# Where the weight preparation stands between two experts: second weight behind all row transposes, last row's split behind the next comparison, sums of squares later

## The chip, the core and the metric

The kernel runs on one core of one Trainium2 chip. Five engines of the core work side by side, each through its own list of instructions in a fixed order: TensorE (PE, matrix products; the load of its stationary operand is listed as PEld), VectorE (DVE), ScalarE (ACT), GpSimd (POOL) and SyncE (SP). DMA queues move data; here SP issues the weight loads and the transposes, POOL the gathers and scatters by row. The metric is the device time of one execution in microseconds (us). An instruction that must wait holds up everything behind it in its engine's list.

## What is computed

Attention of 8 batches with 8 heads over 576 positions comes first; its result, 4608 tokens of 512 values, then goes through a layer of 8 experts. Each expert takes the 576 tokens that a greedy choice over all logits gives to it, and computes two matrix products:

```python
def _moe_ref(x, w_gate, w1, w2):          # N, D, E, F = 4608, 512, 8, 1024
    logits = x @ w_gate
    order = np.argsort(-logits.flatten())
    ...                                    # walk down the order: a token goes to the first expert with room
    for e in range(E):                     # cap = N // E = 576 tokens each
        mask = assigned == e
        h = np.maximum(x[mask] @ w1[e], 0.0)
        out[mask] = h @ w2[e]
```

## The kernel before

The kernel first does the attention (its instructions are not touched by the change), writes the tokens to a scratch tensor in HBM, and then takes the experts one after another, in the order in which they fill. Call these **rounds** 0 to 7 (`ph` in the code), and the change from round k-1 to round k **turn k**. To keep float32 accuracy, every operand is cut into two float16 parts: a high part (ACT copies it, `w1h`, `w2h`, the first half of `xg`) and a low part (DVE subtracts, `w1l`, `w2l`, the second half of `xg`), and each product is done as three.

**One round on PE** (`ffn`): eight groups of 24 matmuls 128x288 (`hidden`, L1208) give the hidden layer, eight tiles of 128 features; each is evicted by ACT (`hh`, L1215) and DVE (`hl`, L1216). Then five tiles of tokens go through the second product (L1256, and L1250 for the last 64 tokens), 24 matmuls 128x512 each; ACT or DVE scale them (`y`) and POOL scatters the rows to the output (L1267).

**What is made ready meanwhile for the next rounds.** Which tokens an expert takes is found by a search in seven steps (`search`): DVE compares all logits with 17 bounds (`cm`, L844), PE counts (L860), DVE adds up (`red`, `r8`, L863 and L866), PE and DVE narrow the bounds (L869, `g1`; L879, `cand18`). Then `slots` and `indices` make the list of token numbers (`idx`, L1000). `tokens` has POOL gather five tiles of rows (`xr`, L1109; 4 x 128 rows and 64), `halve` cuts each into two halves (`xg`, ACT L1098 and DVE L1099), and SP issues one transposing DMA per tile (`xt`, L1100). PE needs `xt` at the start of the round: the first matmul of a pair reads tokens 0 to 287, the second tokens 288 to 575, so that the second needs all five transposes.

**Weights** (`weights`): each round loads `w1` (4 loads of 512 KB) and `w2` (4 more, the `later` function) through SP; ACT squares each quarter and sums it (`square`, `jk`, L1032); `scale` makes a power of two of the sum by way of a PE matmul (L1040, L1042, `ss_e`, `w_sw`); then eight pieces of each are cut into high and low (`split`, L1052 on ACT and L1053 on DVE).

**What sets the order.** Each engine's order is fixed when the program is built. The generators that make ready the next rounds are `chains` with due times in planned nanoseconds: `ffn` yields the planned cost of each matmul, and chains whose time has come put their next step between the matmuls (`T_SQ`, `T_SCALE`, `T_CUT` and so on are the spaces). PE keeps that order; DVE and ACT are ordered by a scheduler after priorities (`urgent`) and readiness in its own model. `follow` adds a constraint of order without a wait: `bulk` keeps a row's DVE split behind the sum (`sums`) of the search step before, and `counted` puts such splits behind the sum that comes next.

Of the kernel before, what the change touches and what calls it, by code (L numbers as in the profile page):

```python
# [13 lines left out]
OP = mybir.AluOpType  # L14
# [44 lines left out]
T_HOT6, T_CLOSE6 = 3200, 9000  # L59
T_W21, T_SCALE2, T_CUT2 = (3200, 300, 3000, 3000), 2600, 1250  # L60
T_F, T_LOAD0, T_HOT1, T_W, T_SQ, T_SCALE, T_CUT, T_BULK0 = 3000, 1500, 6350, 4000, 1500, 1500, 1500, 600
CUT0, T_BEHIND, ROWS_BEHIND = 1, 1300, 3
EDGE0, PEAKS, PEAKS_N = 18, (24, 29), (1, 3)
FIRST_AT = (3, 4)
LATE_Q, STORE_Q = (2, 3), (3, 4, 5)
# [73 lines left out]
def band_stride_attention_then_capacity_moe(ctx, tc, qt, kl, ks, nl, ns, wg, w1, w2, cst, out, dbg=None):  # L139
# [598 lines left out]
    def urgent(ph=1):  # L738
        return tc.high_priority(offset=URGENT * (2 if ph == 0 else 1))

    lately, sums = [], []

    def bulk(ph, ins):
        if ph and ph not in rush:
# [1 line left out]
            lately.append((due_now(), ins))  # L746

    def counted(red, total):
        while lately:
            t, ins = lately.pop()  # L750
            if t > due_now() - T_BEHIND:
                follow(ins, (red, total))
        sums.append(total)

    def spread(ph, todo):
        for step, f in todo:
            if ph not in rush:
                yield step if ph else min(step, T_BULK0)
            f()
# [76 lines left out]
    def search(rm, ohc, more):  # L836
        cand, src, top = cand0, rm, None
        ohv = ohc.rearrange("p c e -> p (c e)")
        for rd in range(R1):
            last = rd == R1 - 1  # L840
            t = cand[:, :J1] if last else cand[:, 1:J1 + 1]
            with urgent():
                cm = rt.tile([TP, NC, J1], F16, name="cm")
                nc.vector.tensor_tensor(cm, src[:, :, None].to_broadcast([TP, NC, J1]),  # L844
                                        t[:, None, :].to_broadcast([TP, NC, J1]), op=OP.is_ge)
                cv = cm.rearrange("p c j -> p (c j)")
                n = 1 if rd == R1 - 2 else J1 + 1
                if not last:
                    pre = cand[:, 0:1]
                    if n > 1:  # L850
                        pre = rt.tile([128, n], F32, name="pre1")
                        nc.vector.tensor_scalar(pre, steps[:, rd + 1, :n], cand[:, 0:1], None, op0=OP.add)
                if rd == 0:
                    more()
            yield pace(T_COUNT) + (X1 if len(closed) == 1 else T_FIRST if rd == 0 else 0)
            with urgent():
                pr = ps_r.tile([128, 512], F32, name="pr_")
                pc, p2, pm = pr[:GC * J1, :GC * E], pr[:, 64:64 + E], pr[:, 128:128 + (E if last else 1)]
                for k in range(0, NC, GC):
                    nc.tensor.matmul(pc, cv[:, k * J1:(k + GC) * J1], ohv[:, k * E:(k + GC) * E], start=(k == 0),  # L860
                                     stop=(k == NC - GC))
                red = rt.tile([GC * J1, GC, E], F16, name="red")
                first_ = nc.vector.tensor_tensor(red.rearrange("p c e -> p (c e)"), pc, fold[:, :GC * E], op=OP.mult)  # L863
                r8 = rt.tile([GC * J1, E], F16, name="r8")
                with nc.allow_low_precision(reason="whole numbers up to 1152"):
                    counted(first_, nc.vector.tensor_reduce(r8, red.rearrange("p c e -> p e c"), axis=AX.X, op=OP.add))  # L866
            yield pace(T_SUM)
            with urgent():
                nc.tensor.matmul(p2, fold[:, GC * E:], r8, start=True, stop=True, skip_group_check=True)  # L869
                g = rt.tile([128, E], F16, name="g1")  # L870
                ih = rt.tile([128, 1], F16, name="ih1")
                if last:
                    nc.vector.tensor_scalar(g, p2, float(CAP), None, op0=OP.is_ge)
                else:
                    with nc.allow_low_precision(reason="zero or one"):
                        nc.vector.tensor_scalar(g, p2, float(CAP), 0.0, op0=OP.is_ge, op1=OP.max, accum_out=ih)
            yield pace(T_STEP)
            with urgent():
                nc.tensor.matmul(pm, ones_j, g if last else ih, start=True, stop=True, skip_group_check=True)  # L879
                if not last:  # L880
                    cand = rt.tile([128, n], F32, name=f"cand{n}")
                    nc.vector.scalar_tensor_tensor(cand, steps[:, rd, J1 + 1:].to_broadcast([128, n]), pm, pre,
                                                   op0=OP.mult, op1=OP.add)
                if rd == R1 - 2:
                    top, src = cand, rt.tile([TP, NC], F32, name="rml")
                    nc.vector.tensor_scalar(src, rm, top, None, op0=OP.subtract)
                    cand = steps[:, rd + 1, :J1 + 1]
        with urgent():
            return settle(pm, top, steps[:, R1 - 1, J1 + 1:])
# [113 lines left out]
    def weights(ph, ei):  # L1003
        e = nc.sync.value_load(ei[0:1, 0:1], min_val=0, max_val=E - 1)
        res, todo = [], []
        for name, w, nch, width, bits in (("w1", w1, DC, FF, W1_BITS), ("w2", w2, FC, DM, W2_BITS)):
# [43 lines left out]
            def split(c, f, k, wf=wf, sc=sc, hi=hi, lo=lo):  # L1050
                s_ = sc.bitcast(F32)[:, 0:1]
                nc.scalar.activation(hi[:, c, f], wf[:, c, f], AF.Copy, scale=s_)  # L1052
                nc.vector.scalar_tensor_tensor(lo[:, c, f], wf[:, c, f], s_, hi[:, c, f], op0=OP.mult,  # L1053
                                               op1=OP.subtract)

            todo.append([(T_SQ, lambda c=c, g=square: g(c)) for c in range(4)])
            todo.append([(T_SCALE, scale)])
# [3 lines left out]
        if ph == 0:  # L1061
# [15 lines left out]
                return g  # L1077

            return res, (start, more, later)
        g = spread(ph, [(T_W, lambda: None)] + sq1 + sc1 + cut1)  # L1080
        chains.append([due_now(), g])
        thirds[ph] = evenly([(t, f) for t, (_, f) in zip(T_W21, sq2)] + [(T_SCALE2, sc2[0][1])] + [(T_CUT2, f) for _, f in cut2])
        return res, g, later
# [10 lines left out]
    def halve(ph, xt, xr, t, n):  # L1094
        xg = xp.tile([128, 2 * DM], F16, name="xg", bufs=5)
        xs, xv = xg[:n].rearrange("q (a j d) -> q j a d", a=2, j=2), xr[:n].rearrange("q (a d) -> q a d", a=2)
        with urgent(ph):
            nc.scalar.activation(xs[:, 0], xv, AF.Copy)  # L1098
            bulk(ph if t < ROWS_BEHIND else 0, nc.vector.tensor_tensor(xs[:, 1], xv, xs[:, 0], op=OP.subtract))  # L1099
            turned.append(nc.sync.dma_start_transpose(xt[:, :, t * 128:t * 128 + n], xg[:n]))  # L1100

    def tokens(ph, idx):
# [84 lines left out]
    def fetch(ph, slot, wts):  # L1187
        idx, sx = yield from indices(ph, slot)
        xt, todo = tokens(ph, idx)
        for t, f in enumerate(todo):  # L1190
            yield T_ROWS if t == 0 else T_ROW
            f()
            if t >= NT - 3:
                wts[2]({NT - 3: (0,), NT - 2: (1,), NT - 1: (2, 3)}[t])
        yield T_LOAD - T_ROWS
        work[ph] = wts[0], xt, idx, sx, wts[1]
        ready.add(ph)
# [84 lines left out]
    def due_now():  # L1282
        return clock
# [10 lines left out]
    with tc.manual_schedule(engines=MAN):  # L1294
        work[0] = now[:4] + (now[4](),)
        chains.append([T_LOAD0, load0()])
        for ph in range(E):
            with tc.manual_schedule(engines=MAN0) if ph in MANP else nullcontext():
# [3 lines left out]
                    advance(c)  # L1302
                rush.add(ph)
                lately.clear()
                for c in list(chains):
                    if c[1] is work[ph][4]:
                        c[0] = clock
                        advance(c)
# [74 lines left out]
```

## Time and profile before

| | |
|---|---|
| time, median of 3 runs | 675.93 us (670.42, 675.93, 676.23) |
| the profiled execution's own time | 676.45 us |
| its span, first to last instruction | 674.7 us |
| PE busy (matmuls) | 603.6 us, 89% of the span |
| DVE, ACT, POOL busy | 454.7, 332.6 and 108.7 us |
| mean granted TensorE clock | 0.957 |
| attention and choice for the first expert | up to about 222 us |
| rounds 0 to 7 | about 222 to 664 us, 54 to 57 us a round from round 1 on |

A busy share is an average over the span. What ends a wait of PE in a round is read from the waits and from the timeline around each turn. The clock of PE is granted in stretches: 1.00 or 0.50 of full speed.

### The profile page before, as it was taken

How to read it: one execution, taken by the hardware profiler on the slowest of the kernel's cores; microseconds unless marked ns; L12 is line 12 of the kernel's file. 1: busy time of each engine (PE TensorE's matmuls, PEld its weight loads, DVE VectorE, ACT ScalarE, POOL GpSimd, SP SyncE). 2: the span in 40 equal slices, each digit the busy share in tenths (PEclk: the TensorE clock that was granted, in tenths of full speed). 3: DMA queues.
4: the chain of work that ended last, by engine and by line, in shares of the span. 5: the costliest groups of instructions: out<-in, count | busy, mean ns of one | idle time of the engine just before them, and what ended most of it. 6: DMA issues, size and time to landing. Idle time of an engine off the chain costs nothing.

```text
span 674.7 us, 19417 instructions
## 1 busy us (share of the span) xinstructions
PE 603.6 (89%) x8128; PEld 395.4 (59%) x8128; DVE 454.7 (67%) x1381; ACT 332.6 (49%) x554; POOL 108.7 (16%) x124
## 2 busy tenths in 40 slices
PE   8789999998947699979999989989998999899993
PEld 4566667766733565457457448547646746646741
DVE  4757778877777888729768776975965956650600
ACT  2555554545302564535655456554565456843510
POOL 2001101111101100400330150051052031211011
PEclk9879999999966899979999999999999999899998
DMA  9868888887314503840590493375257089641010
GB/s 240 202 211 228 233 230 238 248 223 214 111 38 177 167 1 141 193 128 14 181 254 15 149 200 113 141 158 162 111 128 224 20 233 332 142 149 48 1 40 32
DMA packets 76363, 102.40 MB, mean 152 GB/s; under 512 B 41292, under 2 KB 49062, under 8 KB 75763
## 3 DMA queue, kind: packets, MB, share of 16 engines
q1 hardware_dynamic: 68195, 79.61, 41.7%
q0 software_dynamic: 7360, 21.15, 10.7%
q8 instruction: 64, 1.05, 0.7%
q10 hardware_dynamic: 720, 0.39, 0.2%
q14 instruction: 24, 0.20, 0.1%
HBM read 73.60 MB, written 18.87 MB: 137 GB/s over the span
## 4 chain that ended last, share of the span: by engine, by line
PE 17%; issue 15%; DVE 15%; DMA 10%; POOL 4%; ACT 4%; SPq 0%; POOLq 0%; DVEq 0%; ACTq 0%
PE ph L1208 12%; DMA w<-in_w_dram 5%; DVE w2l L1053 3%; PE ph L1256 3%; POOL xr L1109 3%; DMA xr<-x_scr,idx 3%; DVE hl L1216 2%; DVE w1l L1053 2%; DMA xt<-xg 2%; DVE cm L844 1%; ACT jk L1032 1%; POOL out_dram L1267 1%; DVE xg L1099 1%; ACT hh L1215 1%; DMA out_dram<-y,idx 1%
## 5 line engine op out<-in xcount | busy, mean ns | idle before, releaser
L1208 PE MATMUL ph<-xt,w1h 128*128 128x288 f16 (+2 forms) x1024 | 178.9, 290 | 6.8 <-DMA xt<-xg 4.8
L1208 PEld LDWEIGHTS <-w1h 128*128 128x128 f16 x1024 | 97.9, 99 | 36.2 <-issue 5.7
L1208 PE MATMUL ph<-xt,w1l 128*128 128x288 f16 (+2 forms) x512 | 112.1, 290 | 0.0
L1267 POOL DMA_INDIRECT out_dram<-y,idx x40 | 47.3, 1181 | 339.5 <-ACT y L1266 317.5
L1256 PE MATMUL ph<-w2l,hh 128*128 128x512 f16 x256 | 96.9, 379 | 0.4 <-DVE w2l L1053 0.4
L1256 PE MATMUL ph<-w2h,hh 128*128 128x512 f16 x256 | 97.0, 379 | 0.0
L1256 PE MATMUL ph<-w2h,hl 128*128 128x512 f16 x256 | 97.0, 379 | 0.0
L1032 ACT ACTIVATE jk<-w 128x1024 f16<-128x1024 f32 x64 | 67.4, 1054 | 56.5 <-DMA w<-in_w_dram 55.3
L1215 ACT ACTIVATE hh<-ph 128x576 f16<-128x576 f32 (+2 forms) x72 | 42.7, 592 | 81.9 <-PE ph L1208 81.1
L1256 PEld LDWEIGHTS <-hh 128*128 128x128 f16 x512 | 49.1, 98 | 57.4 <-issue 6.7
L1216 DVE SCALAR_TENSOR_TENSOR hl<-ph,hh 128x576 f16<-128x576 f32 (+2 forms) x72 | 49.5, 687 | 47.6 <-ACT hh L1215 47.3
L1208 PEld LDWEIGHTS <-w1l 128*128 128x128 f16 x512 | 50.7, 99 | 14.1 <-issue 1.4
L378 ACT ACTIVATE pr<-spa 128x576 f32<-128x576 f32 x32 | 20.8, 651 | 61.9 <-PE spa L375 45.2
L1053 DVE SCALAR_TENSOR_TENSOR w1l<-w,w_sw,w1h 128x512 f16<-128x512 f32 x64 | 46.1, 745 | 4.8 <-ACT w1h L1052 4.8
L1109 POOL DMA_INDIRECT xr<-x_scr,idx x40 | 41.5, 1038 | 46.8 <-DVE L L953 25.3
L1052 ACT ACTIVATE w1h<-w,w_sw 128x512 f16<-128x512 f32 x64 | 42.2, 710 | 13.0 <-DVE w_sw L210 11.9
L1266 ACT ACTIVATE y<-ph,so 128x512 f32<-128x512 f32 x32 | 21.8, 681 | 53.4 <-PE ph L1256 53.3
L1053 DVE SCALAR_TENSOR_TENSOR w2l<-w,w_sw,w2h 128x512 f16<-128x512 f32 x64 | 46.8, 746 | 0.4 <-ACT w2h L1052 0.3
L1052 ACT ACTIVATE w2h<-w,w_sw 128x512 f16<-128x512 f32 x64 | 42.2, 711 | 8.1 <-DVE w_sw L210 8.1
L1256 PEld LDWEIGHTS <-hl 128*128 128x128 f16 x256 | 24.9, 97 | 29.8 <-issue 4.0
L429 POOL DMA_DIRECT2D x_scr<-xs x23 | 15.1, 661 | 159.2 <-DVE vsum L298 101.7
L1099 DVE TENSOR_TENSOR xg<-xr,xg 128x512 f16<-128x512 f32 (+1 forms) x37 | 24.8, 685 | 15.1 <-ACT xg L1098 14.9
(619 smaller groups left out, 929.7 us busy)
## 6 DMA issues: line engine op xcount, KB each, us to landing
w<-in_w_dram SPq DMA_DIRECT2D x64, 512.0 KB
kl<-in_kl_dram SPq DMA_DIRECT2D x16, 304.0 KB
v_s<-in_ns_dram SPq DMA_DIRECT2D x16, 292.5 KB
v_l<-in_nl_dram SPq DMA_DIRECT2D x16, 292.5 KB
ks<-in_ks_dram SPq DMA_DIRECT2D x16, 288.0 KB
qs<-in_qt_dram SPq DMA_DIRECT2D x16, 288.0 KB
ql<-in_qt_dram SPq DMA_DIRECT2D x16, 288.0 KB
x_scr<-xl SPq DMA_DIRECT2D x8, 512.0 KB
```

The source lines that it names most:

```text
L378: nc.scalar.activation(pr[:, :S].rearrange("k (h n) -> k h n", h=2), u.sp[p][:, :, :HS], AF.Exp, scale=0.125)
L1032: ins = nc.scalar.activation(jk, wf[:, c * n4:(c + 1) * n4].rearrange("p c f -> p (c f)"), AF.Square, scale=1.41422, accum_out=sq[:, c:c + 1])
L1052: nc.scalar.activation(hi[:, c, f], wf[:, c, f], AF.Copy, scale=s_)
L1053: nc.vector.scalar_tensor_tensor(lo[:, c, f], wf[:, c, f], s_, hi[:, c, f], op0=OP.mult, op1=OP.subtract)
L1099: bulk(ph if t < ROWS_BEHIND else 0, nc.vector.tensor_tensor(xs[:, 1], xv, xs[:, 0], op=OP.subtract))
L1109: nc.gpsimd.indirect_dma_start(out=xr[:n], out_offset=None, in_=x_rows, in_offset=bass.IndirectOffsetOnAxis(ap=idx[:n, t:t + 1], axis=0))
L1208: nc.tensor.matmul(tile_[:, j, :w], wt[:, d, f * 128:(f + 1) * 128], xt[:, d // 2, xx, d % 2, c], start=(k == 0), stop=(k == 3 * DC - 1))
L1215: evicted.append(nc.scalar.activation(hv, src, AF.Relu))
L1216: nc.vector.scalar_tensor_tensor(lv, src, 0.0, hv, op0=OP.max, op1=OP.subtract)
L1256: nc.tensor.matmul(py, a[:, f, ts_], w[:, f], start=(k == 0), stop=(k == len(todo) - 1))
L1266: nc.scalar.activation(y, py, AF.Copy, scale=so[:, t:t + 1])
L1267: st = nc.gpsimd.indirect_dma_start(out=out_rows, out_offset=bass.IndirectOffsetOnAxis(ap=idx[:n, t:t + 1], axis=0), in_=y[:n], in_offset= ...
```

## The change

Four edits:

1. `fetch` issues all four loads of `w2` behind the fifth transpose. Before, they were handed out one behind the third, one behind the fourth and two behind the fifth transpose.
2. `halve`, rounds 1 to 6: the DVE split of the last row tile (64 rows) is put behind the comparison `cm` that was built last.
3. `split`, rounds not yet begun: the DVE pieces from number 6 on (5 on in round 1, counted from 0) of each weight go behind the last sum of the search, and those of them that are at most 4000 planned ns old (`T_TAIL`) behind the next sum too.
4. The scale of `w1` stands 2800 planned ns behind its last square instead of 1500, and in round 7 the squares of `w1` begin 15000 instead of 4000 planned ns after the weight is asked for.

```diff
-CUT0, T_BEHIND, ROWS_BEHIND = 1, 1300, 3
+CUT0, T_BEHIND, ROWS_BEHIND, PIECES, T_TAIL, T_SCALE1, T_W7 = 1, 1300, 3, 6, 4000, 2800, 15000
...
     def counted(red, total):
+        while pieces:
+            t, ins = pieces.pop()
+            if t > due_now() - T_TAIL:
+                follow(ins, (total,))
         while lately:
...
-                nc.vector.tensor_tensor(cm, src[:, :, None].to_broadcast([TP, NC, J1]),
-                                        t[:, None, :].to_broadcast([TP, NC, J1]), op=OP.is_ge)
+                cms.append(nc.vector.tensor_tensor(cm, src[:, :, None].to_broadcast([TP, NC, J1]),
+                                                 t[:, None, :].to_broadcast([TP, NC, J1]), op=OP.is_ge))
...
-                nc.vector.scalar_tensor_tensor(lo[:, c, f], wf[:, c, f], s_, hi[:, c, f], op0=OP.mult,
-                                               op1=OP.subtract)
+                ins = nc.vector.scalar_tensor_tensor(lo[:, c, f], wf[:, c, f], s_, hi[:, c, f], op0=OP.mult,
+                                                     op1=OP.subtract)
+                if ph and ph not in rush and k >= PIECES - (ph == 1):
+                    follow(ins, sums[-1:])
+                    pieces.append((due_now(), ins))
...
-        g = spread(ph, [(T_W, lambda: None)] + sq1 + sc1 + cut1)
+        g = spread(ph, [(T_W if ph < E - 1 else T_W7, lambda: None)] + sq1 + [(T_SCALE1, sc1[0][1])] + cut1)
...
-            bulk(ph if t < ROWS_BEHIND else 0, nc.vector.tensor_tensor(xs[:, 1], xv, xs[:, 0], op=OP.subtract))
+            ins = nc.vector.tensor_tensor(xs[:, 1], xv, xs[:, 0], op=OP.subtract)
+            if t < ROWS_BEHIND:
+                bulk(ph, ins)
+            elif 0 < ph < E - 1 and t == NT - 1:
+                follow(ins, cms[-1:])
...
             f()
-            if t >= NT - 3:
-                wts[2]({NT - 3: (0,), NT - 2: (1,), NT - 1: (2, 3)}[t])
+        wts[2](range(4))
...
                 lately.clear()
+                pieces.clear()
```

No instruction is added or taken out. What moves is shown at three places. Line numbers of the changed kernel are 4 higher from `search` on, 7 at the row split, 10 or 11 from the transposes to the end.

**Turn 1, SP.** The transposes of round 1's rows and the loads of its second weight (`w_4794`). Before:

```order
L1100 DMA_TRANSPOSE xt<-xg 128x8x128 x3
L1012 ISA
L1012 DMA w_4794<-in_w_dram 128x2x512
L1100 DMA_TRANSPOSE xt<-xg 128x8x128
L1012 ISA
L1012 DMA w_4794<-in_w_dram 128x2x512
L1100 DMA_TRANSPOSE xt<-xg 128x8x64
```

Now:

```order
L1111 DMA_TRANSPOSE xt<-xg 128x8x128 x4
L1111 DMA_TRANSPOSE xt<-xg 128x8x64
L1016 ISA
L1016 DMA w_4794<-in_w_dram 128x2x512
L1016 ISA
L1016 DMA w_4794<-in_w_dram 128x2x512
```

Two loads have left the gaps between the last three transposes. At turns 2 to 5 all five transposes already stood ahead of the loads.

**Turn 3 (turns 2, 4 and 5 read alike), ACT and DVE.** `w1h` and `w1l` are the pieces of the next round's first weight, `xg` the row tiles, `cm` the next comparison of the search. Before, ACT and then DVE:

```order
L1052 ACTIVATE w1h<-w_6317,w_sw_6323 128x4x128 x5
L1266 ACTIVATE y<-ph,so 128x512
L1098 ACTIVATE xg<-xr 128x2x256 x4
L1052 ACTIVATE w1h<-w_6317,w_sw_6323 128x4x128
L1098 ACTIVATE xg<-xr 64x2x256
```

```order
L1099 TENSOR_TENSOR xg<-xr,xg 128x2x256 x2
L876 TENSOR_SCALAR g_6630,ih_6631<-pr__6602 128x8
L1099 TENSOR_TENSOR xg<-xr,xg 128x2x256 x2
L882 SCALAR_TENSOR_TENSOR cand_6646<-steps,pr__6602,pre_6578 128x18
L1099 TENSOR_TENSOR xg<-xr,xg 64x2x256
L844 TENSOR_TENSOR cm<-rmn,cand_6646 128x612
```

Now, ACT (the piece of the list at turn 3) and then DVE:

```order
L1056 ACTIVATE w1h<-w_6317,w_sw_6323 128x4x128 x3
L1276 ACTIVATE y<-ph,so 128x512
L1105 ACTIVATE xg<-xr 128x2x256 x4
L1105 ACTIVATE xg<-xr 64x2x256
L1056 ACTIVATE w1h<-w_6317,w_sw_6323 128x4x128 x4
```

```order
L1106 TENSOR_TENSOR xg<-xr,xg 128x2x256 x3
L880 TENSOR_SCALAR g_6630,ih_6631<-pr__6602 128x8
L1106 TENSOR_TENSOR xg<-xr,xg 128x2x256
L1057 SCALAR_TENSOR_TENSOR w1l<-w_6317,w_sw_6323,w1h 128x4x128
L886 SCALAR_TENSOR_TENSOR cand_6644<-steps,pr__6602,pre_6578 128x18
L1057 SCALAR_TENSOR_TENSOR w1l<-w_6317,w_sw_6323,w1h 128x4x128
L848 TENSOR_TENSOR cm<-rmn,cand_6644 128x612
L856 TENSOR_SCALAR pre_6648<-steps,cand_6644 128x18
L1106 TENSOR_TENSOR xg<-xr,xg 64x2x256
```

On DVE the last row tile has gone behind the comparison, and two pieces of `w1l` (numbers 3 and 4) have come ahead of it; on ACT three pieces of `w1h` stand ahead of the rows instead of five, and pieces 3 and 4 now stand behind the last row tile.

**Round 6, ACT.** `w_8621` is round 6's own second weight, `w_8977` round 7's first. Before:

```order
L1032 ACTIVATE jk,sq<-w_8621 128x1024 x2
L1032 ACTIVATE jk,sq<-w_8977 128x1024
L1215 ACTIVATE hh<-ph 128x576
L1032 ACTIVATE jk,sq<-w_8621 128x1024
L1032 ACTIVATE jk,sq<-w_8977 128x1024 x2
L1215 ACTIVATE hh<-ph 128x576
L1032 ACTIVATE jk,sq<-w_8621 128x1024
```

Now:

```order
L1036 ACTIVATE jk,sq<-w_8621 128x1024 x2
L1225 ACTIVATE hh<-ph 128x576
L1036 ACTIVATE jk,sq<-w_8621 128x1024
L1225 ACTIVATE hh<-ph 128x576
L1036 ACTIVATE jk,sq<-w_8621 128x1024
L1036 ACTIVATE jk,sq<-w_8977 128x1024 x2
L1225 ACTIVATE hh<-ph 128x576
```

The squares of round 7's first weight no longer stand between those of the weight that is needed in this round; on PE the two scale matmuls (L1042), 3 matmuls apart before, are now 93 matmuls apart.

More of the change, by code (lines that the diff above doesn't have):

```diff
@@ L739, in urgent @@
         return tc.high_priority(offset=URGENT * (2 if ph == 0 else 1))
-    lately, sums = [], []
+    lately, sums, cms, pieces = [], [], [], []
     def bulk(ph, ins):
```

## The prediction

> **What bounds the kernel now.** I read first the page's busy shares, then the waits of PE in rounds 1 to 6 (columns: us in total, times, longest).
>
> ```profile
> PE 603.6 (89%) x8128; PEld 395.4 (59%) x8128; DVE 454.7 (67%) x1381; ACT 332.6 (49%) x554; POOL 108.7 (16%) x124
> ...
> PE ph L1208 <- DMA xt<-xg: 4.8, 3, 4.2
> PE pr__6684 L860 <- DVE cm L844: 2.1, 1, 2.1
> PE pr__8214 L860 <- DVE cm L844: 2.0, 1, 2.0
> PE pr__9204 L1042 <- DVE ss L1040: 1.9, 1, 1.9
> PE pr__7449 L860 <- DVE cm L844: 1.7, 1, 1.7
> ...
> PE pr__5919 L860 <- DVE cm L844: 0.9, 1, 0.9
> PE ph L1256 <- DVE w2l L1053: 0.4, 1, 0.4
> ...
> PE pr__6684 L869 <- DVE r L866: 0.3, 1, 0.3
> ...
> PE pr__9152 L996 <- DVE p L991: 0.3, 1, 0.3
> ```
>
> PE carries the rounds; nothing but its own waits can be won or lost there. They stand at three kinds of place: 4.8 us for the transposed rows (nearly all at turn 1), 6.7 us in all for the comparison `cm` (turns 2 to 5: 0.9, 2.1, 1.7, 2.0), and 1.9 + 0.3 + 0.4 us in round 6. Each edit aims at one of them. A wait has a second price, the clock. Windows of 3.41 us, with PE's busy time and its granted clock (first and second number behind the length):
>
> ```profile
> 286.05:289.46 3.41, 0.04 (x1) 1.00 1.10 290
> 289.46:292.88 3.42, 2.55 (x11) 0.50 1.07 403
> 292.88:296.29 3.41, 3.41 (x23) 0.50 0.00 0
> 395.28:398.69 3.41, 1.45 (x7) 1.00 1.14 202
> ...
> 504.50:507.92 3.42, 1.43 (x7) 1.00 1.17 247
> 576.18:579.60 3.42, 1.48 (x15) 1.00 0.71 204
> 579.60:583.01 3.41, 3.41 (x16) 0.50 0.75 196
> ```
>
> After the empty window at turn 1 two windows ran at half clock, after 1.48 us busy in round 6 one; after 1.45 us at turn 3 and 1.43 us at turn 5 none. So around 1.45 us of work, about 2 us of idling, in a window lies the edge, and it isn't sharp. A busy window at half clock loses 3.41 / 2 = 1.7 us.
>
> **Turn 1: the loads behind all transposes.** SP's list, PE's waits, and the chain's pieces for the fifth transpose of turns 1, 2 and 3 (start, us from its issue until PE may go on):
>
> ```profile
> 276.91 5.27 SPq L1100 DMA_TRANSPOSE xt<-xg  x3
> 282.37 1.18 SPq L1012 DMA_DIRECT2D w<-in_w_dram  x1
> 283.65 1.32 SPq L1100 DMA_TRANSPOSE xt<-xg  x1
> 285.17 0.44 SPq L1012 DMA_DIRECT2D w<-in_w_dram  x1
> 285.71 1.34 SPq L1100 DMA_TRANSPOSE xt<-xg  x1
> ...
> 290.33 0.90 PE L1208 MATMUL ph<-xt,w1h 128*128 128x288 f16 x3 [4.23 <-DMA xt<-xg]
> ...
> 285.71 4.57 DMA xt<-xg
> ...
> 344.35 2.84 DMA xt<-xg
> 399.32 3.81 DMA xt<-xg
> ```
>
> The third transpose's issue ends at 276.91 + 5.27 = 282.18. Without the loads the fourth follows at about 282.3, and 1.32 us later, at 283.7, the fifth: 2.0 us sooner than 285.71. From issue to PE it took 4.57 us with loads in between, 2.84 and 3.81 at turns 2 and 3, where no load stands ahead: 286.5 to 287.5. POOL's scatters share these microseconds, so I take 287.5, a gain of 290.33 - 287.5 = **2.8 us**; the other ends are 2.0 (still 4.57 us) and 3.8. PE then idles about 2 us instead of 4.8, right at the edge of the clock. Before, 290.33 to 296.29 ran at half clock, 6.0 us for 3.0 us of work. I take one half window left instead of two: **-1.3 us** (ends 0 and -3.0). The loads come up to 3 us later; their cover is the first product: ACT's list has the squares of `w2` behind the eviction of hidden tiles, and PE has 192 matmuls to run before it uses `w2`.
>
> **Turns 2 to 5: the last row behind the comparison.** Turn 3 in rows, ACT, then DVE, then PE:
>
> ```profile
> 386.43 3.17 ACT L1052 ACTIVATE w1h<-w,w_sw 128x512 f16<-128x512 f32 x5 [2.22 <-DVE w_sw L210]
> 396.77 0.63 ACT L1098 ACTIVATE xg<-xr 64x512 f16<-64x512 f32 x1 [1.29 <-DMA xr<-x_scr,idx]
> ...
> 386.36 0.17 DVE L1000 TENSOR_SCALAR idx<-idx 128x5 int32<-128x5 int32 x1
> 387.19 0.75 DVE L1053 SCALAR_TENSOR_TENSOR w1l<-w,w_sw,w1h 128x512 f16<-128x512 f32 x1 [0.66 <-ACT w1h L1052]
> 387.86 0.24 DVE L882 SCALAR_TENSOR_TENSOR cand<-steps,pr__6477,pre 128x18 f32<-128x18 f32 x1
> 388.01 0.74 DVE L1053 SCALAR_TENSOR_TENSOR w1l<-w,w_sw,w1h 128x512 f16<-128x512 f32 x1
> 388.67 0.79 DVE L844 TENSOR_TENSOR cm<-rmn,cand 128x612 f16<-128x612 f32 x1
> 397.44 0.68 DVE L1099 TENSOR_TENSOR xg<-xr,xg 64x512 f16<-64x512 f32 x1 [1.69 <-ACT xg L1098]
> 398.04 0.78 DVE L844 TENSOR_TENSOR cm<-rmn,cand 128x612 f16<-128x612 f32 x1
> ...
> 398.88 0.47 PE L860 MATMUL pr__6684<-ohn,cm 128*68 128x32 f16 x9 [2.15 <-DVE cm L844]
> ```
>
> The comparison ended at 398.82, 1.42 us behind the end of the last row's ACT copy at 397.40, which waited for the gather. The row's DVE split no longer stands between them. But the order now has two pieces of `w1l` ahead of the comparison, and their `w1h` stands on ACT **behind** the same last row copy. Both engines run their lists in order, so the comparison waits for the last gather still, and by a longer way: copy, `w1h`, `w1l`, `cand`, `w1l`, `cm`. That way stands in the rows once already: from `w1h` at 386.43 to the end of `cm` at 388.67 + 0.79 = 389.46 it took 3.03 us; the first `w1h` starts 0.09 us ahead of the copy's modelled end. So `cm` ends 2.94 instead of 1.42 us behind the copy: +1.5 us.
>
> The gather itself starts earlier. The three `ss_e` and `w_sw` stood ahead of the token list on DVE and now stand behind it, and the scale matmul behind PE's use of `p`; with some 0.16 us each I take the list 0.4 us earlier (ends 0 and 0.6). So `cm` comes +1.1 us, and PE's wait grows to about 1.6, 2.9, 2.4 and 2.7 us less or more 0.3 (the arrival of PE at the place is earlier, too). Behind it, the 0.3 us wait at L869 for `r` goes, since `red` and `r8` now have no `w1l` between them: 1.1 - 0.35, **+0.75 us a turn**. The last transpose is then issued 0.8 us behind `cm`, at 400.8 in turn 3, and lands 2.84 to 3.81 us later, at 403.6 to 404.6; PE would want it at 403.2 + 0.75 = 403.9. So up to 0.7 us more, at turn 3 alone, where the 3.81 stands; I add 0.2. Sum of four turns: 4 x 0.75 + 0.2 = **+3.2 us** (ends +1 and +5; if gathers land 3 us sooner than in this trace, below nothing: rival 3).
>
> The clock: at turns 3, 4 and 5 PE now idles 2.4 to 2.9 us in one piece, beyond the 2 us of the edge when most of it falls into one window, and for 2.7 us in a 3.41 us window that is the case some two times in three. Two windows at half clock: **+3.4 us** (ends 0 and 5.1).
>
> Here a rule speaks on the other side. The Trainium skill, "TensorE: Matmul & The Clock Gate", Part 1 (the HAM clock gate), says that the clock is throttled after at least one idle window of about 3.4 us. By it no wait at turns 2 to 5 costs clock, nor the one left at turn 1: rival 1 below. The trace doesn't bear the rule out fully: a window with 1.48 us of work was followed by half clock.
>
> **Round 6: the squares apart.** ACT and PE:
>
> ```profile
> 570.93 1.06 ACT L1032 ACTIVATE jk<-w 128x1024 f16<-128x1024 f32 x1 [2.30 <-DMA w<-in_w_dram]
> ...
> 579.02 0.18 PE L1042 MATMUL pr__9204<-ss,ones_b 128*128 128x1 bf16 x1 [1.94 <-DVE ss L1040]
> ...
> 592.02 0.38 PE L1256 MATMUL ph<-w2h,hh 128*128 128x512 f16 x1
> ...
> 582.25 1.15 ACT L1098 ACTIVATE xg<-xr 128x512 f16<-128x512 f32 x2 [1.02 <-DMA xr<-x_scr,idx]
> ```
>
> The square at 570.93 is one of round 7's; it waited 2.30 us for its load and held up all that stands behind it on ACT. By the order it and two more squares of round 7, 1.06 us each, stood ahead of the fourth square of `w2` and go behind it: up to 2.30 + 3 x 1.06 = 5.5 us less ahead of the sum for which PE waited 1.94. So the waits of 1.94 and 0.32 us go, and the half window behind them, 1.7 us. The second product could start at 592.02 - 4.0 = 588.0. What is late next is `w2h`: its scale stands on DVE behind the last row, and on ACT behind two squares of `w1`, until about 586.5: the row copies end at 582.25 + 1.15 = 583.4, then come an eviction (as long as a row copy, 0.6), two squares of 1.06 and another eviction. Eight pieces at 3.17 / 5 = 0.63 us on ACT, some 0.7 on DVE, and two evictions end near 594; PE's first token tile starts at 588.0 and would want the last piece some 5 us later, at 593. So I count 1 us of waits for `w2l` instead of 0.4. Net 4.0 - 0.6 = **-3.4 us** (ends -1.5 and -4.0). Round 7's first weight is cut behind that, with 96 more matmuls of the second product and the 24 of the last tile ahead of its use.
>
> **Sum**, against the profiled execution's 676.45 us: -2.8 - 1.3 + 3.2 + 3.4 - 3.4 = -0.9, so 675.5. That execution lies 0.5 us above the median of 675.93, so I say **675.0 us**. A change within 1% (6.8 us) is about what a measurement of this kernel can't tell from none.
>
> **Rivals.** 1: the clock holds at all ends: -2.8 - 3.0 + 3.2 - 3.4 = -6.0, 670 us. For it: the windows with 1.43 and 1.45 us busy kept it; against it: round 6. The skill's rule gives this time. Chance 0.25.
> 2, slower: half clock after every long wait, turn 1 keeps its two windows, and at turns 3 to 5 two windows each follow, as after the empty window at 286.05. The point is a window with clearly less than 1.45 us of work; then 3 x 3.0 = +9 for +3.4 and nothing for turn 1's -1.3: 675.5 + 5.6 + 1.3 = 682 us, and 684 if the fifth transpose lands late at all four turns. Chance 0.12.
> 3: the gathers land so early that the order works as its words say and `cm` never waits for the last row. Then turns 2 to 5 give -6.7 - 1.4 instead of +3.2 + 3.4: 661 us. Against it: the last gather took until 396.75 while PE arrived at 396.7, and nothing in front of it gains 3 us. Chance 0.08.
> 4: the transposes of turn 1 are held by the DMA engines, not by SP's list (2.0 us instead of 2.8 and no clock gained), and round 6 wins its waits alone: 679 us. Chance 0.1.
>
> **From these the numbers.** My forecast, 672 to 678 us, has 0.45; the range 667 to 682 leaves out rival 3 and the upper half of rival 2. Faster by over 1% (below 669.2): rival 3 and a third of rival 1 and some of the forecast's tail, 0.18. Slower by over 1% (above 682.7): 0.08.
>
> **What would show it.** Right: at turn 1 the wait for `xt` is 2 to 2.5 us; at turns 2 to 5 the wait of L860 for `cm` is 1.5 to 3 us and the DVE row ahead of `cm` is `w1l`, waiting for ACT `w1h`; L1042 waits nowhere in round 6, and the second product there starts near 588 less the shift of all before. Wrong: if L860's waits at turns 3 to 5 have shrunk, the chain through ACT is not what I take it for; if half clock appears after each, the range is too low.

## The result, and the profile after

| | before | changed |
|---|---|---|
| median of 22 runs, us | 676.02 (667.24 to 684.81) | 680.59 (674.36 to 692.66) |
| ratio of times (see below) | | 1.012 (95% interval 1.009 to 1.015) |
| the profiled execution's own time, us | 676.45 | 679.91 |

The change made the kernel slower, by 4.6 us in the medians and by 1.2%, or 8 us, in the ratio. The ratio leaves out executions that lie more than 1.5% above the fastest of their kernel, so it need not agree with the medians, which keep all of them. The forecast was 675.0 us, a hair faster than before, with a range of 667 to 682: the measured median lies in that range, but on the other side of the kernel before. Single runs spread over 18 us; what each edit did is therefore read from its own place in the profile, and times decide only between sums of several places.

PE's waits in the changed kernel from round 0's end to round 6 (us in total, times, longest):

```profile
PE pr__7445 L864 <- DVE cm L848: 4.6, 1, 4.6
PE pr__6680 L864 <- DVE cm L848: 4.5, 1, 4.5
PE pr__8210 L864 <- DVE cm L848: 3.3, 1, 3.3
PE pr__5915 L864 <- DVE cm L848: 3.1, 1, 3.1
PE ph L1218 <- DMA xt<-xg: 1.5, 1, 1.5
PE ph L1266 <- DVE hl L1226: 1.2, 1, 1.2
PE pr__6602 L883 <- DVE g L880: 1.2, 1, 1.2
PE pr__7367 L883 <- DVE g L880: 1.2, 1, 1.2
```

The transposed rows are waited for 1.5 us instead of 4.8, and the wait for `ss` in round 6 is gone. But the four waits for `cm` grew from 6.7 to 15.5 us, and waits for `g` are new. The starts of the two products in each round, from the first matmul of each in the two traces, show where the time went:

| stretch | before | changed | difference | forecast |
|---|---|---|---|---|
| turn 1's end: first product of round 1 | 32.6 | 27.0 | -5.6 | -4.1 |
| turn 2: second product of round 1 to the start of round 2 | 28.3 | 31.9 | +3.5 | +0.75 |
| turn 3, in the same way | 30.3 | 34.0 | +3.7 | the four turns |
| turn 4 | 28.8 | 35.1 | +6.3 | together +6.6, |
| turn 5 | 29.3 | 30.5 | +1.2 | clock included |
| round 6 | 53.6 | 51.7 | -1.8 | -3.4 |

Turns 2 to 5 cost 14.8 us, more than twice the forecast, and outweigh turn 1 and round 6. The stretches of the table sum to +7.4 us, while the two profiled executions differ by 3.5: the other 3.9 us, by which the changed kernel is faster, lie outside these stretches, 2.4 of them ahead of round 0's second product, up to where DVE, ACT and POOL have the same order in both kernels. Those 2.4 us are no work of the change.

**Turn 1** went as forecast. SP's list and PE's first wait, in the changed kernel:

```profile
275.70 7.03 SPq L1111 DMA_TRANSPOSE xt<-xg  x4
282.92 2.15 SPq L1016 DMA_DIRECT2D w<-in_w_dram  x4
284.29 0.54 PE L1218 MATMUL ph<-xt,w1h 128*128 128x288 f16 x3 [1.48 <-DMA xt<-xg]
```

The four transposes follow each other with no load between them. One wait of 1.48 us is left where 4.23 stood.

**Turn 3**, in the changed kernel: POOL's issue of the last gather, then ACT, DVE and PE.

```profile
386.24 1.08 POOL L1120 DMA_INDIRECT xr<-x_scr,idx  x1 [0.30 <-issue]
...
392.17 0.63 ACT L1105 ACTIVATE xg<-xr 64x512 f16<-64x512 f32 x1 [2.49 <-DMA xr<-x_scr,idx]
392.71 2.54 ACT L1056 ACTIVATE w1h<-w,w_sw 128x512 f16<-128x512 f32 x4
...
393.45 0.75 DVE L1057 SCALAR_TENSOR_TENSOR w1l<-w,w_sw,w1h 128x512 f16<-128x512 f32 x1 [3.04 <-ACT w1h L1056]
394.11 0.24 DVE L886 SCALAR_TENSOR_TENSOR cand<-steps,pr__6602,pre 128x18 f32<-128x18 f32 x1
394.27 0.74 DVE L1057 SCALAR_TENSOR_TENSOR w1l<-w,w_sw,w1h 128x512 f16<-128x512 f32 x1
394.93 0.79 DVE L848 TENSOR_TENSOR cm<-rmn,cand 128x612 f16<-128x612 f32 x1
...
388.08 0.16 PE L883 MATMUL pr__6602<-ih,ones_j 128*128 128x1 f16 x1 [1.20 <-DVE g L880]
...
395.77 0.63 PE L864 MATMUL pr__6680<-ohn,cm 128*68 128x32 f16 x9 [4.49 <-DVE cm L848]
```

DVE stood still for 3.04 us ahead of `w1l`, which waited for `w1h`, which stood behind the copy of the last row, which waited for its gather. That is the forecast chain. From the copy's end at 392.80 to the end of `cm` at 395.72 it took 2.92 us; 2.94 were forecast. What the forecast did not have is above it. The gather took 5.93 us from its issue to its copy (386.24 to 392.17). Before, the POOL row was this, and the copy came at 396.77, 4.72 us later:

```profile
392.05 1.26 POOL L1109 DMA_INDIRECT xr<-x_scr,idx  x1 [0.30 <-issue]
```

At turn 3 POOL also came to it 1.0 us later behind the token list (6.5 us instead of 5.5; so too at turn 4, not at turns 2 and 5). From the list to the end of `cm` it took 2.9, 3.7, 4.3 and 2.1 us longer than before at turns 2 to 5. And PE waited 1.20 us for `g`, because three row splits now stand ahead of it on DVE where two stood, and each waits for its gather.

**The clock.** Windows of 3.41 us in the changed kernel, PE's busy time, granted clock:

```profile
283.27:286.68 3.41, 2.39 (x20) 1.00 0.87 182
334.47:337.88 3.41, 1.52 (x15) 1.00 0.84 169
337.88:341.30 3.42, 3.42 (x12) 0.50 0.82 220
392.50:395.91 3.41, 0.14 (x4) 1.00 0.74 160
395.91:399.32 3.41, 3.41 (x18) 0.50 0.46 106
450.52:453.94 3.42, 0.03 (x1) 1.00 1.31 189
453.94:457.35 3.41, 2.17 (x13) 0.50 0.29 64
457.35:460.76 3.41, 3.41 (x10) 0.50 0.96 235
508.55:511.96 3.41, 1.85 (x9) 1.00 1.17 180
511.96:515.38 3.42, 1.68 (x16) 1.00 0.74 143
```

Four half windows at turns 2, 3 and 4 with 3.42 + 3.41 + 2.17 + 3.41 us of busy PE, half of it lost: 6.2 us. The window of turn 1's wait (2.39 us busy) brought none. The wait of 3.3 us at turn 5 was cut in two by a window's border (1.85 and 1.68 us busy) and cost none.

These parts come near the 14.8: waits for `cm` +8.8, for `g` +3.5, half clock +6.2, waits for `r` and `p` that went -2.7, in sum 15.8. The 1.0 us between is not accounted for.

### The profile page after: what moved, and what is told of

Read it like the earlier page. It is cut to its first block, busy times and chain, and to the rows that moved or that the text cites. A ratio compares the mean times of both kernels' runs of the same rounds, so it can differ in the third digit from the quotient of the medians.

```text
span 678.1 us, 19409 instructions
## 1 busy us (share of the span) xinstructions
PE 602.1 (89%) x8125; PEld 393.4 (58%) x8128; DVE 456.4 (67%) x1381; ACT 332.1 (49%) x554; POOL 107.0 (16%) x124
## 4 chain that ended last, share of the span: by engine, by line
PE 28%; issue 14%; DVE 11%; DMA 5%; POOL 4%; ACT 3%; SPq 0%; POOLq 0%; DVEq 0%; ACTq 0%
PE ph L1218 14%; PE ph L1266 10%; DMA xr<-x_scr,idx 3%; POOL xr L1120 3%; DVE w2l L1057 3%; DMA w<-in_w_dram 2%; DVE hl L1226 2%; PE ph L1260 2%; POOL out_dram L1277 1%; DVE cm L848 1%; DVE w1l L1057 1%; ACT hh L1225 1%; ACT w2h L1056 1%; ACT jk L1036 1%; ACT w1h L1056 0%
## 5 line engine op out<-in xcount | busy, mean ns | idle before, releaser
L1218 PE MATMUL ph<-xt,w1h 128*128 128x288 f16 (+2 forms) x1024 | 174.4, 286 | 3.6 <-DMA xt<-xg 1.5
L1218 PE MATMUL ph<-xt,w1l 128*128 128x288 f16 (+2 forms) x512 | 110.0, 286 | 0.0
L1266 PE MATMUL ph<-w2h,hh 128*128 128x512 f16 x256 | 99.1, 387 | 1.2 <-DVE hl L1226 1.2
L1266 PE MATMUL ph<-w2l,hh 128*128 128x512 f16 x256 | 99.4, 388 | 0.7 <-DVE w2l L1057 0.7
L1277 POOL DMA_INDIRECT out_dram<-y,idx x40 | 44.6, 1114 | 347.5 <-ACT y L1276 327.4
L1266 PE MATMUL ph<-w2h,hl 128*128 128x512 f16 x256 | 99.1, 387 | 0.3 <-DVE ss_e L205 0.3
```

Source lines behind the costliest of these rows:

```text
L1218: nc.tensor.matmul(tile_[:, j, :w], wt[:, d, f * 128:(f + 1) * 128], xt[:, d // 2, xx, d % 2, c], start=(k == 0), stop=(k == 3 * DC - 1))
L1266: nc.tensor.matmul(py, a[:, f, ts_], w[:, f], start=(k == 0), stop=(k == len(todo) - 1))
L1277: st = nc.gpsimd.indirect_dma_start(out=out_rows, out_offset=bass.IndirectOffsetOnAxis(ap=idx[:n, t:t + 1], axis=0), in_=y[:n], in_offset= ...
```

## Experiments

**1. The two edits that were forecast as gains, alone.** The kernel before with

```diff
-            if t >= NT - 3:
-                wts[2]({NT - 3: (0,), NT - 2: (1,), NT - 1: (2, 3)}[t])
+        wts[2](range(4))
...
-        g = spread(ph, [(T_W, lambda: None)] + sq1 + sc1 + cut1)
+        g = spread(ph, [(T_W if ph < E - 1 else T_W7, lambda: None)] + sq1 + sc1 + cut1)    # T_W7 = 15000
```

> The kernel before with two of the edits alone: the second weight's loads behind all five transposes, and round 7's squares begun 15000 instead of 4000 planned ns after their weight is asked for. Turns 2 to 5 keep the order of before. My theory: the two edits that were forecast as gains are gains, and everything lost stands at turns 2 to 5. Then the wait of PE for xt at turn 1 is about 1.5 us as in the changed kernel (4.2 before) with no half clock behind it, the waits for ss and p in round 6 are gone, and PE's waits for cm at turns 2 to 5 stay at 0.9 to 2.2 us: 676 - 3.1 - 3.0 - 2.8 = 667 us. Rival: what is won at the two places comes back as half clock at the turns that lie at its edge (windows with 1.4 us of work), so 671 to 674 us.

Measured: 668.89 us against 675.66, ratio 0.987 (0.979 to 0.994). PE's waits, of a profiled execution that took 672.83 us:

```profile
PE ph L1207 <- DMA xt<-xg: 2.8, 2, 1.9
PE pr__5917 L860 <- DVE cm L844: 2.0, 1, 2.0
PE pr__8212 L860 <- DVE cm L844: 1.6, 1, 1.6
PE pr__6682 L860 <- DVE cm L844: 1.5, 1, 1.5
...
PE pr__7447 L860 <- DVE cm L844: 0.9, 1, 0.9
```

0.95 us of the wait for `xt` stand at turn 1. The waits for `cm` are those of before, and no half clock followed any of them. So these two edits win some 7 us together in the medians (9 by the ratio, 4 to 14); the remaining edits lose more than that.

**2. The scale put back, the rest of the change left.** The changed kernel with

```diff
-CUT0, T_BEHIND, ROWS_BEHIND, PIECES, T_TAIL, T_SCALE1, T_W7 = 1, 1300, 3, 6, 4000, 2800, 15000
+CUT0, T_BEHIND, ROWS_BEHIND, PIECES, T_TAIL, T_SCALE1, T_W7 = 1, 1300, 3, 6, 4000, 1500, 15000
```

> The changed kernel with one number put back: the scale of the first weight 1500 instead of 2800 planned ns behind its last square. All else of the change stays. By the order five pieces of w1h stand ahead of the rows on ACT again, one piece of w1l stands ahead of cm on DVE, and its w1h is ahead of the last row copy. My theory: cm then no longer hangs on the last gather. It ends some 1.6 us behind the fourth row's split, PE waits 0.5 us for it instead of 3.1 to 4.6, and the last transpose, issued 0.8 us behind cm, is waited for up to 1 us at the start of the round: about 664 us in all. Rival one: the last rows, split behind cm, are what the round's start then waits for, 1.5 to 2 us at each turn, and the clock falls as often: 670 us or more. Rival two: the edits 2 and 3 themselves cost the time, not this number: 678 to 681 us.

Measured: 669.05 us, ratio 0.988 (0.983 to 0.993). PE's waits:

```profile
PE ph L1218 <- DMA xt<-xg: 10.4, 6, 2.8
...
PE pr__5917 L864 <- DVE cm L848: 0.6, 1, 0.6
```

The waits for `cm` at turns 2 to 5 fell to 0.60, 0.31, 0.47 and 0.57 us, as expected. But PE waits for `xt` at the starts of rounds 2 to 5 instead, 1.9, 3.4, 1.0 and 2.8 us. So the time came out 5 us above my figure: rival one had the sizes, and one half window fell into it. The scale's 1300 planned ns account for the loss; with them back, the change is worth as much as the first experiment's two edits, so what is left of edits 2 and 3 adds nothing that these runs can tell.

**3. The scale alone.** The kernel before with 2800 instead of 1500 planned ns ahead of the scale of each `w1`:

```diff
-        g = spread(ph, [(T_W, lambda: None)] + sq1 + sc1 + cut1)
+        g = spread(ph, [(T_W, lambda: None)] + sq1 + [(2800, sc1[0][1])] + cut1)
```

> The kernel before with one number changed: the scale of the first weight 2800 instead of 1500 planned ns behind its last square. Loads, last row and round 7's squares as before. By the order one piece of w1l, whose w1h stands on ACT behind the last row copy, comes ahead of cm, and two pieces fewer stand on DVE ahead of the first row splits. My theory: this number alone brings most of the loss. cm ends 2.0 us behind the last row copy's end instead of 1.4, PE waits 1 us for g behind the third row at the turns, as in the changed kernel, and the last gather takes 1.4 us longer from its issue to the copy (about 5 us where it took 3.4 to 4.7), because the row splits, and with them three transposes instead of two, run ahead of its packets: waits for cm of 2.2 to 3.7 us and three half windows, 676 + 9 = 685 us. Rival: the gather lands as before, and PE waits 1.3 to 2.7 us for cm: 676 + 3 to 5 = 680 us.

Measured: 687.55 us against 675.66, ratio 1.011 (1.003 to 1.020). At turn 3, POOL, ACT and DVE (its profiled execution took 690.72 us):

```profile
394.38 1.11 POOL L1109 DMA_INDIRECT xr<-x_scr,idx  x1 [0.30 <-issue]
...
401.06 0.63 ACT L1098 ACTIVATE xg<-xr 64x512 f16<-64x512 f32 x1 [3.19 <-DMA xr<-x_scr,idx]
...
403.14 0.78 DVE L844 TENSOR_TENSOR cm<-rmn,cand 128x612 f16<-128x612 f32 x1
```

`cm` ends 2.23 us behind the copy (2.0 expected), the last gather takes 6.68 us, and PE waits 2.3, 4.5, 3.8 and 2.5 us for `cm` (2.2 to 3.7 expected), with half windows at turns 3 to 5. By the ratio this number alone loses 7.6 us (2 to 13); the medians lie 12 us apart. Together with the first experiment's gain that makes +5 us by the medians, where the changed kernel has 4.6, but -1.5 by the ratios, give or take 8, where it has 8. So the times alone don't show that gain and loss simply add up. The profile shows the place: the four stretches of turns 2 to 5 took 131.1 us here, 131.4 in the changed kernel and 116.6 before.

**4. The first three transposes held back.** In rounds 2 to 6 of the changed kernel the fourth row's transpose is issued first, the other three behind it:

```diff
-            turned.append(nc.sync.dma_start_transpose(xt[:, :, t * 128:t * 128 + n], xg[:n]))
+            held.append((xt[:, :, t * 128:t * 128 + n], xg[:n]))
+            if ph < 2 or t >= 3:
+                for k, (o_, i_) in enumerate(held[-1:] + held[:-1]):
+                    turned.append(nc.sync.dma_start_transpose(o_, i_))
+                    if k:
+                        follow(turned[-1], turned[-2:-1])
+                held.clear()
```

> The changed kernel; in rounds 2 to 6 the transpose of the fourth row tile is issued first, and those of the first three behind it, so that none runs while the first gathers are under way. My theory: the last gather of turns 2 to 5 lands late since transposes run ahead of it on the same DMA engines. Then from its issue to its row copy it takes 3.4 to 4.5 us instead of 4.9 to 6.1, the comparison comes 1 to 1.5 us sooner, PE's waits for cm fall from 3.1 to 4.6 us to 2 to 3.3, and with fewer half windows the time falls by 4 to 9 us, to 672 to 677 us. Rival: the gather's time is its own or that of the scatter behind it; then it stays at 4.9 to 6.1 us, and the kernel at 680 us or, if the transposes crowd at the round's start, above.

Measured: 682.08 us, ratio 1.008 (1.004 to 1.013). At turn 3, POOL, ACT and SP, and PE's waits for `xt` over rounds 1 to 6:

```profile
391.89 1.11 POOL L1126 DMA_INDIRECT xr<-x_scr,idx  x1 [0.30 <-issue]
...
395.04 0.63 ACT L1105 ACTIVATE xg<-xr 64x512 f16<-64x512 f32 x1 [0.45 <-DMA xr<-x_scr,idx]
...
395.38 7.54 SPq L1114 DMA_TRANSPOSE xt<-xg  x5
...
PE ph L1224 <- DMA xt<-xg: 10.6, 9, 2.7
```

From the last gather's issue to its copy, by the same rows of turns 2, 3, 4 and 5 in each kernel, in us:

| kernel | turn 2 | 3 | 4 | 5 |
|---|---|---|---|---|
| before | 3.4 | 4.7 | 4.3 | 4.6 |
| changed | 4.9 | 5.9 | 6.1 | 5.2 |
| scale alone | 5.0 | 6.7 | 5.9 | 6.4 |
| transposes held | 3.4 | 3.2 | 3.2 | 3.2 |

So the transposes that run beside it are what delays the last gather. SP's transposes of turn 3, before and in the changed kernel, whose last gathers were issued at 392.05 and 386.24:

```profile
392.58 7.97 SPq L1100 DMA_TRANSPOSE xt<-xg  x5
...
385.18 13.12 SPq L1111 DMA_TRANSPOSE xt<-xg  x5
```

Before, the first of them came 0.5 us behind the last gather's issue; now it comes 1.1 us ahead of it. By the order, that is because the row splits no longer have two pieces of `w1l` ahead of them on DVE. The Trainium skill, "DMA: Bandwidth & Descriptors", Queues, rings and completion order, says that each DMA engine takes turns between the queues that have work for it. The table fits that (3.2 to 3.4 us with no transpose under way, 4.9 to 6.1 beside them in the changed kernel); the turns themselves no run here shows. The waits for `cm` fell to 1.5, 1.6, 1.4 and less than 0.3. The mechanism was as expected, the time (672 to 677 us) was not: the five transposes now stand at the end, and PE waits 10.6 us for `xt`. The wait moved from one place to another.

**5. The pieces of `w1l` behind the next sum.** The changed kernel with PIECES 3 instead of 6:

```diff
-CUT0, T_BEHIND, ROWS_BEHIND, PIECES, T_TAIL, T_SCALE1, T_W7 = 1, 1300, 3, 6, 4000, 2800, 15000
+CUT0, T_BEHIND, ROWS_BEHIND, PIECES, T_TAIL, T_SCALE1, T_W7 = 1, 1300, 3, 3, 4000, 2800, 15000
```

> The changed kernel with PIECES 3 instead of 6: the low pieces of each first weight from number 3 on go behind the sum that comes next, so that by the order nothing but cand stands between the fourth row's split and cm on DVE at turns 2 to 5. ACT keeps the order of the changed kernel, three pieces of w1h ahead of the rows. My theory: it is the two pieces of w1l between them that tie cm to the last gather. Then PE's waits for cm at turns 2 to 5 fall from 3.1 to 4.6 us to 0 to 0.3, though the last gather lands as late as in the changed kernel (4.9 to 6.1 us from its issue to its copy), the waits for g of 0.6 to 1.2 us stay, and the last transpose is waited for 0.5 to 3 us at the start of the rounds: 666 to 671 us. Rival: cm is late for the fourth gather or for g, with the pieces only riding along; then the waits stay above 2 us and the time at 677 us or more.

Measured: 666.36 us against 675.42, ratio 0.984 (0.979 to 0.989). Turn 3 (POOL, ACT, DVE) and PE's waits:

```profile
383.15 1.05 POOL L1120 DMA_INDIRECT xr<-x_scr,idx  x1 [0.30 <-issue]
...
388.71 0.63 ACT L1105 ACTIVATE xg<-xr 64x512 f16<-64x512 f32 x1 [2.29 <-DMA xr<-x_scr,idx]
...
387.33 0.80 DVE L848 TENSOR_TENSOR cm<-rmn,cand 128x612 f16<-128x612 f32 x1
...
PE ph L1218 <- DMA xt<-xg: 5.8, 6, 2.2
PE pr__5837 L883 <- DVE g L880: 1.2, 1, 1.2
...
PE pr__5915 L864 <- DVE cm L848: 0.3, 1, 0.3
```

The gather is as late as in the changed kernel (5.56 us here), but `cm` ran at 387.33, ahead of the last row's copy, and PE waits 0.3 us for it at turn 2, as long at turn 5, and not at turns 3 and 4. All came about as expected. One number separates this kernel from the changed one, and 14 us in the medians. At turns 2 to 5 it moves three pieces of `w1l` on DVE, the two ahead of `cm` and the next, and at turn 1 a piece and the last row; the orders of ACT and POOL are the same. It shows that the pieces ahead of `cm` are the cause. It is the fastest kernel measured, though its interval overlaps with those of experiments 1, 2, 7 and 8.

**6 and 9. PE kept at work.** The changed kernel with matmuls of zeros ahead of the count, 12 of them and then 26:

```diff
                 pr = ps_r.tile([128, 512], F32, name="pr_")
+                for _ in range(12 if rd == 2 and 3 <= len(closed) <= 6 else 0):    # 26 in the second
+                    nc.tensor.matmul(pr[:, 256:], warm_i[:, :128], warm_i[:, :256], start=True, stop=True,
+                                     skip_group_check=True)
```

> The changed kernel, and on PE twelve matmuls of zeros, 128x256 each, ahead of the count for which PE waits at turns 2 to 5: work without use, about 2.4 us, in the idle time of 3.1 to 4.6 us. Nothing waits for less. My theory: the half clock behind these waits comes from the idle window alone. Then PE starts the count when it did, the half windows at turns 2 to 5 (four in the profile of the changed kernel, 6.2 us of lost work) go, and the time is 674 to 676 us. Rival: the clock there doesn't follow the idling of PE in the window before, or the work of zeros counts for nothing: 680 us as the changed kernel, or 682 to 685 if it delays the count.

> The same as the kernel with twelve matmuls of zeros ahead of the count at turns 2 to 5, now with 26 of them: the twelve took 0.11 us each, 1.3 us, and left 2.2 to 3.5 us of idling; 26 are 2.8 us and leave 0.3 to 1.8 us. Two of four half windows went with twelve, those behind windows with 0.42 and 0.55 of a window's work; those behind 0.14 and 0.35 stayed. My theory: about 0.45 of a window, 1.5 us of work, decides, and with 26 matmuls every window at turns 2 to 5 has more: no half window there, PE's wait including the zeros as long as in the changed kernel (3.1 to 4.6 us), and about 680.6 - 6 = 674 to 676 us. Rival: the clock follows something else than PE's work in the window before; then two or more half windows stay at turns 2 to 5 and the time at 680 us.

Measured: 680.20 us, ratio 1.007 (1.001 to 1.012), and 680.86 us, ratio 1.011 (1.005 to 1.017). Windows with twelve, and behind the dots with 26:

```profile
330.12:333.54 3.42, 0.48 (x6) 1.00 1.04 201
333.54:336.95 3.41, 3.41 (x17) 0.50 0.44 96
388.15:391.56 3.41, 1.45 (x13) 1.00 1.19 116
446.18:449.59 3.41, 1.18 (x17) 1.00 1.18 199
...
338.58:341.99 3.41, 1.50 (x18) 1.00 0.53 113
341.99:345.40 3.41, 3.41 (x11) 0.50 0.68 165
```

Both expectations of 674 to 676 us were missed. Half windows at turns 2 to 5 did fall, from four to two and to one, and with them the work lost to half clock there, from 6.2 us to 3.4 and 1.7. But PE's waiting at these turns, with the zeros (1.5 and 3.0 us a turn) counted as waiting, grew by some 2 us in both, so the four stretches took 131.1 and 128.9 us instead of 131.4. One place where the zeros themselves cost time is in the trace of the second: at turn 4 they held the count until 457.08, while `cm` had ended at 455.81. In the timed runs it reads alike: the mean granted clock is 0.955 in the changed kernel, 0.960 with twelve and 0.964 with 26, and the time is the same. What took the place of the half clock in those runs was not found.

**7. The last row ahead of `cm` again.** Experiment 2's kernel without edit 2:

```diff
             if t < ROWS_BEHIND:
                 bulk(ph, ins)
-            elif 0 < ph < E - 1 and t == NT - 1:
-                follow(ins, cms[-1:])
```

> The changed kernel with two edits undone: the scale of the first weight at 1500 planned ns again, and the last row's split no longer behind cm. Left are the loads, the low pieces from number 6 on behind the sums, and round 7's squares. Against the kernel with the scale alone put back (669.05 us) it shows what the last row's place is worth. My theory: it moves a wait and removes none. PE's waits for cm are 0.9 to 2 us at turns 2 to 5 instead of 0.3 to 0.6, and those for xt at the starts of rounds 2 to 5 fall from 1 to 3.4 us to 0 to 1.9: 667 to 670 us, no difference that can be told from that kernel's. Rival: the comparison is what counts, and the time rises by 4 x 1.2 = 5 us, to 674 us.

Measured: 667.95 us, ratio 0.989 (0.984 to 0.994). Waits for `cm` 1.0, 2.2, 1.9 and 2.0 us, for `xt` at the starts of rounds 2 to 5 1.5, 0, 0.3 and 0; half windows stand at turns 3 and 5. The last row's place moves the wait and removes none, as expected. One more row of this profile matters for edit 1: at turn 1, with the loads behind all transposes as in the changed kernel, PE waited 1.36 and 2.35 us for `xt`, and a half window followed. So what edit 1 wins there is not the same in every kernel; why was not tried.

**8. One piece less ahead of `cm`.** Experiment 2's kernel with PIECES 5 instead of 6, in the same line as above.

> The changed kernel with the scale of the first weight at 1500 planned ns again and PIECES 5 instead of 6: by the order no low piece stands between the fourth row's split and cm at turns 2 to 5, and the last row's split follows directly behind cm. Against the kernel with the scale alone put back, cm and the last split come one piece, 0.66 us, sooner. My theory: the waits for cm of 0.3 to 0.6 us go, those for xt at the starts of the rounds shrink by 0.6 us each, and no half clock is left at the turns: 669 - 2 - 2.4 - 1 = 664 us. Rival: the transposes wait for SP and the DMA engines, not for the split; then xt comes as late as before and PE waits at the start of the round for what it doesn't wait for at cm: 668 to 669 us.

Measured: 670.40 us, ratio 0.989 (0.984 to 0.995). No wait for `cm` at turns 2 to 5 is left, but PE waits 3.0, 3.7, 1.4 and 1.5 us for `xt`, and one half window stands at turn 3. The rival was right: what is won at `cm` is paid at `xt`.

**All of turns 2 to 5 in one number.** From the first matmul of round 1's second product to that of round 5's, in the profiles (one execution of each kernel):

| kernel | us |
|---|---|
| before | 218.8 |
| experiment 1 (loads and round 7's squares) | 218.8 |
| changed | 232.9 |
| experiment 3 (scale alone) | 232.6 |
| experiments 2, 5, 7, 8 | 221.5, 220.8, 221.8, 219.9 |

None of these is better there than the kernel before. Those that win against it win outside these turns, where experiment 1's edits act; at the turns they only take back the loss.

## Why the prediction was wrong, point by point

- **Turn 1, the wait**: right. -2.8 us forecast, 4.23 + 0.36 to 1.48 us measured, -3.1. **The clock there**: one half window too many was kept; none was left (-3.0 instead of -1.3). PE was busy for 2.39 us in the window of the wait.
- **Turns 2 to 5, the chain**: right in kind and in length. `cm` hung on `w1l`, `w1h`, the copy and the gather, 2.92 us behind the copy's end (2.94).
- **Turns 2 to 5, the gather**: this is the step that failed, the term "+0.75 us a turn", +3.2 us in sum. "The gather itself starts earlier" was counted as 0.4 us in favour. The list was 0.4 us earlier against the round's start at turns 4 and 5 (38.2 us behind it, 38.6 before), but the gather that followed took 1.5, 1.2, 1.8 and 0.6 us longer. I priced the gather at its old length, though the same order let the splits, and with them the transposes, run ahead into it; and POOL's 1.0 us at turns 3 and 4, whose cause was not tried, were not in it either. Waits for `cm` of 1.6, 2.9, 2.4 and 2.7 us were forecast; 3.1, 4.5, 4.6 and 3.3 came, more by 1.5, 1.6, 2.2 and 0.6, turn by turn about what the gather took longer. (Those four forecasts already have the 0.35 us of the wait for `r` taken off; with `cm` 1.1 us later, as the text before them says, they would be 2.0, 3.2, 2.8 and 3.1. The sum of 0.75 us a turn is not touched by that.)
- **Turns 2 to 5, a wait not seen**: the third row split ahead of `g` held PE 0.55 to 1.20 us a turn, 3.5 in all. While `cm` is the later one this costs nothing of its own, since PE would have waited as much longer for `cm`; in experiment 5 it does. The rows of the order that I had quoted show it (`xg` x3 ahead of `g,ih`, two before); I gave it no price.
- **Turns 2 to 5, the clock**: two half windows forecast, four came, 6.2 us instead of 3.4. Rival 2 had two windows at a turn, which came at turn 4 alone. It tied the second one to the empty window ahead; turn 3's window was nearly empty too (0.14 us busy), and one half window followed. What goes with a second one is said in the last section.
- **Round 6**: the waits for `ss` and `p` went, and the second product came 2.8 us sooner against the round's start. What was late next was `hl` for 1.24 us, not `w2l` alone, and the round gained 1.8 us instead of 3.4; that lies within the ends given, -1.5 and -4.0.
- **Sum**: the forecast set a loss of 6.6 us against a gain of 7.5. The gain was 7.4 by the profiles and about 7 by the medians of experiment 1; the loss was 14.8 by the profiles, and in experiment 3, which has the scale alone, 14.5 by its profile and 8 (ratio) to 12 (medians) by its times. That the forecast sum came out near the kernel before was no more than two terms of opposite sign.

What stays open is how much of the loss in the timed runs is half clock. Experiments 6 and 9 did not settle it. The granted clock of the runs gives its size for the whole kernel: one minus the clock, times the span, is 30.8 us on average in the 22 runs of the changed kernel and 25.8 us in 51 runs of the kernel before, measured beside the experiments. By this estimate half clock takes some 5 us more than before, less what PE stood idle in half windows. The two profiled executions, with 0.957 and 0.958, don't show that difference: the one of before had a lower clock than its kernel's mean of 0.962.

## What to carry to other kernels

An order that moves work behind a wait must be read to its end: the copy on ACT that the moved piece stood ahead of was the one that waited for a gather, and two pieces of weight on DVE tied the comparison to it. When an engine comes free sooner, price what it releases: here three row splits came sooner, their transposes too, and these slowed the gather that the chain ended on. And a wait that several transfers share (the rows' gathers, transposes and the comparison) moves from one place to the next when one of them is hurried: of the kernels with the late scale only the one that took the comparison out of the chain won.

## What the runs showed of the hardware

The half clock has an edge that the eleven traces of this study place rather well. Taken are the windows of 3.41 us at full clock, from the first matmul of round 0 to the end of round 7. Where PE or its weight loads were busy for up to 0.41 of the window, 17 of 17 were followed by half clock; with 0.42 to 0.47, 7 of 15; with 0.48 to 0.70, 1 of 69; with more, none. So a wait costs clock when it leaves less than 1.4 us of work in one of these windows, sometimes with 1.4 to 1.6 us, and hardly ever above. Where the wait lies against the windows' borders decides: 4.5 us of idling in one piece at turn 3 cost one half window, 3.3 us at turn 5 none. The Trainium skill, "TensorE: Matmul & The Clock Gate", Part 1 (the HAM clock gate), lets the clock fall after an idle window; here windows that were two fifths busy brought it too, and the measurement decides.

Whether a second half window follows goes with the work in the first. In the same traces and rounds (one case begins 0.2 us ahead of round 0) the first half window was busy for 0.64 to 0.83 of its length in the 3 cases where a second followed (turn 4 here and turn 1 before are two of them), and for 0.88 or more in the 29 cases where none did.

A gather of 64 rows, issued last at turns 2 to 5, took 3.2 to 3.4 us from issue to copy with no transpose beside it (experiment 4), 3.4 to 4.7 with two or three issued ahead of the copy (before), and 4.9 to 6.7 with four (changed kernel and experiment 3).
